# One split operation on 128 partitions with low halves carried by DMA, and a third staging tile for weight slices

## The chip, the cores and the metric

The kernel runs on one core of a Trainium2 chip. A core has TensorE (PE, matrix multiplication, with its weight loads shown as PEld), VectorE (DVE), ScalarE (ACT), GpSimd (POOL) and SyncE (SP), which here issues the DMA transfers, in the order in which they stand in its queue. Each engine works through its own instructions in order and waits for others through semaphores. On-chip data lies in a memory of 128 partitions; TensorE writes its sums to eight banks of a second memory. The metric is the device time of one execution, in microseconds (us).

## The reference

Attention with a causal mask and a bias that decays with a running sum, then two dense layers with different nonlinearities, in single precision:

```python
# 4 batches, 8 heads, 576 positions, 64 per head
scores = (1.0 / np.sqrt(D)) * np.matmul(q, k.transpose(0, 1, 3, 2))
cum = np.cumsum(np.maximum(s, 0.0), axis=-1)
bias = -(cum[:, :, :, None] - cum[:, :, None, :])
scores = np.where(causal, -1000000000.0, scores + np.minimum(bias, 0.0))
attn = softmax(scores); x = attn @ v          # 2304 tokens x 512
h = x @ w_in;  x = (h * np.cos(h)) @ w_out     # first expert layer, 512 -> 2048 -> 512
h = x @ w_in2; out = (np.maximum(h, 0) + np.log1p(np.exp(-np.abs(h)))) @ w_out2
```

The weights arrive in double precision.

## The kernel before

**Precision.** A product is made of three matmuls on operands that are split into a high half (a rounded copy) and a low half (the value less its high half): high x high, high x low, low x high. Splitting is the work of ScalarE (the copy) and VectorE (the subtraction).

**Attention** runs over 32 units (batch and head). Two neighbouring heads form a pair, which is loaded, split and kept together. `raw` (two buffers) takes the loaded keys on partitions 0 to 63 and queries on 64 to 127. `tbk` gets the keys' high halves on partitions 0 to 63 (L482) and low halves on 64 to 127 (L492), `tbq` the queries' low halves on 0 to 63 (L494) and high halves on 64 to 127 (L483), so one matmul over 128 partitions gives both mixed products. `tak` and `taq` get the high halves again, by DMA (L485, L486), with the running sums as further rows. These tiles lie in three slots inside the tile `wlate`, so the trace calls all of them `wlate`; the first pair is prepared apart. For each unit TensorE first makes scores once for their maxima (L510, VectorE takes masked maxima into `mx`; its other output `junk` is never read), then the scores again for the exponentials (L564), then the products with the values. L538 copies numerators and denominators out, a DMA writes them to `adram`; after every fourth unit the denominators are read back (`rd<-adram`), and VectorE takes their reciprocals (L591, L592), to be used when the expert layers' input is loaded (L620).

**Expert layers.** Tokens are taken in blocks of 512 (one of 256), hidden features in 16 chunks of 128. For a chunk TensorE makes the hidden values in one of four banks (operands `xh`, `xl`), ScalarE and VectorE apply the nonlinearity (L657 to L664 in the first layer, L669 to L676 in the second), the result is split into `ghi` (L298) and `glo` (L307), and TensorE adds the chunk's share of the output in the other four banks. L664 and L676 free a chunk's bank.

**Weights.** Each of the two layers has 32 half slices. A half slice (512 KB in double precision) is loaded into one of two tiles `stage`, and brought to single precision in one of two tiles `conv` by L422 (ScalarE) and L424, L426, L429 and L432 (VectorE); then L440 and L442 split it (shown as L298 and L307 or L308). L432 is the last to read the staging tile.

**What sets the order.** A planner written in Python (class `Planner`) gives each operation a due time `vt`, plays the program through with estimated durations, and so fixes the order on each engine; on the chip each engine keeps that order, whatever the real times are. A transfer's landing is reckoned as its issue, 640 ns, its bytes, and 770 ns more. Where TensorE would have nothing to do at the start, the planner puts warming matmuls on zeros (L376). Due times are in units of attention (`u + offset`, offsets in `TUNE`: split -0.462, maxima -0.4135, scores 1.63) or of chunks.

## Time and profile before

| | us |
|---|---|
| median of three runs | 1023.58 |
| lowest, highest | 1022.13, 1024.79 |
| the profiled execution | 1024.17 |
| its span in the trace | 1022.4 |
| TensorE busy in the span | 1006.6 (98%) |
| VectorE busy | 701.5 (69%) |
| ScalarE busy | 613.8 (60%) |
| GpSimd busy | 49.4 (5%) |
| all DMA | 95.31 MB in 45098 packets |

The span is the time from the first to the last instruction of the program; the execution took 1.8 us more than that. Busy shares of the whole span are means over very different stretches. TensorE's matmuls overlap, and their ends are modelled, so "busy" is not the same as working at its best; where an engine is late shows in the waits. A releaser of a wait is inferred from semaphores.

### The profile page before, as it was taken

What the parts mean: (1) busy time and instruction counts of PE and PEld (TensorE: products, weight loads), DVE (VectorE), ACT (ScalarE), POOL (GpSimd) and SP (SyncE); (2) the same over time, 40 slices, a digit from 0 to 9 for tenths busy, and PEclk for the clock granted to TensorE, in tenths of its full rate; (3) what the DMA queues carried; (4) which work ended last, traced back from release to release, by engine and by line L of the source; (5) the groups of instructions that cost most, each with busy time, mean ns of one, the idle gap of its engine ahead of it and who ended that gap; (6) DMA issues with size and microseconds to landing.
All of it is one profiled execution on the core that took longest, in us unless ns stands there. A gap on an engine that the chain in (4) does not pass through costs nothing.

```text
span 1022.4 us, 14520 instructions
## 1 busy us (share of the span) xinstructions
PE 1006.6 (98%) x5179; PEld 844.5 (83%) x5179; DVE 701.5 (69%) x1441; ACT 613.8 (60%) x1129; POOL 49.4 (5%) x67
## 2 busy tenths in 40 slices
PE   8999999999999999999999998999999999999998
PEld 7888788877888889988888886888888998888886
DVE  8799898969974545545458999975564756545553
ACT  4777777767765545555456668664455555554444
POOL 8112111100000000000000000000000000000000
PEclk9999999999999999999999999999999999999999
DMA  5766666773522222102014435310230200001001
GB/s 164 223 184 201 169 181 189 190 198 114 170 83 83 62 83 82 44 21 62 1 43 136 152 124 175 124 62 1 83 105 9 84 1 23 19 1 42 1 1 41
DMA packets 45098, 95.31 MB, mean 93 GB/s; under 512 B 7586, under 2 KB 14242, under 8 KB 45026
## 3 DMA queue, kind: packets, MB, share of 16 engines
q1 hardware_dynamic: 45026, 94.39, 30.4%
q8 instruction: 40, 0.66, 0.3%
q14 instruction: 32, 0.26, 0.1%
HBM read 66.87 MB, written 18.64 MB: 84 GB/s over the span
## 4 chain that ended last, share of the span: by engine, by line
PE 81%; DMA 8%; DVE 5%; ACT 3%; issue 2%; POOL 1%; SPq 0%; ACTq 0%; DVEq 0%; POOLq 0%
PE bank L321 80%; DMA stage<-w 5%; DMA adram<-num 2%; PE bank L376 1%; DMA rd<-adram 1%; DVE conv L429 1%; ACT conv L422 1%; DVE junk L510 1%; DMA raw<-adram 1%; DVE pf L664 0%; DVE conv L432 0%; DVE conv L426 0%; POOL wlate L329 0%; DVE glo L307 0%; ACT pf L564 0%
## 5 line engine op out<-in xcount | busy, mean ns | idle before, releaser
L321 PE MATMUL bank<-xh,wearly 128*128 128x512 f32 (+1 forms) x640 | 195.5, 371 | 3.8 <-DVE pf L664 3.8
L321 PE MATMUL bank<-ghi,wearly 128*128 128x512 f32 (+1 forms) x640 | 194.9, 370 | 1.3 <-ACT ghi L298 1.3
L321 PE MATMUL bank<-ghi,wlate 128*128 128x512 f32 (+1 forms) x640 | 193.4, 368 | 0.6 <-ACT ghi L298 0.6
L321 PE MATMUL bank<-xh,wlate 128*128 128x512 f32 (+1 forms) x640 | 193.6, 368 | 0.0
L298 ACT ACTIVATE ghi<-pf 128x512 fp32r<-128x512 f32 (+1 forms) x160 | 94.1, 588 | 145.8 <-DVE pf L676 97.5
L307 DVE TENSOR_TENSOR glo<-pf,ghi 128x512 fp32r<-128x512 f32 (+1 forms) x160 | 101.9, 637 | 78.2 <-ACT ghi L298 77.6
L321 PE MATMUL bank<-wlate 128*128 128x320 f32 (+9 forms) x576 | 149.4, 362 | 2.9 <-POOL xl L329 1.7
L321 PEld LDWEIGHTS bank<-xh,wearly 128*128 128x128 f32 x640 | 118.1, 190 | 24.9 <-DVE pf L664 4.5
L321 PEld LDWEIGHTS bank<-ghi,wearly 128*128 128x128 f32 x640 | 118.0, 190 | 21.8 <-ACT ghi L298 1.7
L321 PEld LDWEIGHTS bank<-ghi,wlate 128*128 128x128 f32 x640 | 117.2, 189 | 20.9 <-ACT ghi L298 1.0
L321 PEld LDWEIGHTS bank<-xh,wlate 128*128 128x128 f32 x640 | 117.2, 189 | 19.9
L321 PE MATMUL bank<-pf,vf 128*65 128x320 f32 (+4 forms) x448 | 126.4, 384 | 0.8 <-ACT pf L564 0.8
L321 PE MATMUL bank<-glo,wlate 128*128 128x512 f32 (+1 forms) x320 | 118.1, 369 | 1.2 <-DVE glo L307 1.2
L321 PE MATMUL bank<-glo,wearly 128*128 128x512 f32 (+1 forms) x320 | 118.5, 370 | 0.2 <-DVE glo L307 0.2
L321 PE MATMUL bank<-xl,wearly 128*128 128x512 f32 (+1 forms) x320 | 118.4, 370 | 0.0
L321 PE MATMUL bank<-xl,wlate 128*128 128x512 f32 (+1 forms) x320 | 117.7, 368 | 0.0
L672 DVE SCALAR_TENSOR_TENSOR bc<-pf 128x512 f32<-128x512 f32 (+1 forms) x80 | 51.0, 638 | 86.1 <-ACT pf L670 86.0
L321 PEld LDWEIGHTS bank<-wlate 128*128 128x128 f32 (+1 forms) x576 | 94.6, 192 | 17.9 <-DVE mx L510 2.8
L660 DVE SCALAR_TENSOR_TENSOR pf<-pf,pf 128x512 f32<-128x512 f32 (+1 forms) x80 | 50.8, 635 | 54.8 <-ACT pf L658 54.7
L510 DVE CUSTOM_DVE_ANT_0 junk<-bank,mask 128x384 bf16<-128x384 f32 (+3 forms) x192 | 81.8, 468 | 9.3 <-PE bank L321 7.8
L564 ACT ACTIVATE pf<-bank 128x256 f32<-128x256 f32 (+2 forms) x160 | 67.0, 431 | 33.1 <-PE bank L321 24.7
L669 ACT ACTIVATE pf<-bank 128x512 f32<-128x512 f32 (+1 forms) x80 | 44.3, 554 | 67.7 <-PE bank L321 65.1
(79 smaller groups left out, 1370.2 us busy)
## 6 DMA issues: line engine op xcount, KB each, us to landing
stage<-w SPq DMA_DIRECT2D x64, 512.0 KB
raw<-qk SPq DMA_DIRECT2D x15, 576.0 KB
wlate<-wlate SPq DMA_DIRECT2D x30, 288.0 KB
vf<-v SPq DMA_DIRECT2D x32, 160.0 KB
adram<-num SPq DMA_DIRECT2D x32, 146.2 KB
xdram<-num SPq DMA_DIRECT2D x18, 256.0 KB
out<-num SPq DMA_DIRECT2D x18, 256.0 KB
raw<-adram SPq DMA_DIRECT2D x32, 128.0 KB
```

The lines of the kernel that those rows point to most:

```text
L298: opts.append((ACT, act_t(n, psum), (lambda: A.activation(o, i, AF.Copy, scale=1.0 if scale is None else scale))))
L307: return [(DVE, dve_t(n), lambda: V.tensor_tensor(o, a, hi.bitcast(F32), op=ALU.subtract))]
L321: X.matmul(o, a, b, start=st, stop=sp, skip_group_check=skip)
L376: X.matmul(bank[7][:, 0:256], zero[:, 0:128], zero, start=True, stop=True)
L422: P.op(vs_ - 2, [(ACT, act_t(512), lambda cf=cf, pr=pr: A.activation(cf, pr[:, :, 1].bitcast(F32), AF.Abs))], r=[(("st", i), (tag, half))] ...
L429: P.op(vs_ + 1, [(DVE, dve_t(512), lambda cv=cv, pr=pr: V.scalar_tensor_tensor(cv, pr[:, :, 1], 0xC0000000, cv, op0=ALU.bitwise_and, op1=A ...
L510: P.op(tx + 1, [(DVE, dve_t(w, True) + DX, lambda bk=bk, off=off, w=w, mo=mo, col=col, pr=pr, jk=junk[i if x < 2 else x - 2]: V.tensor_ten ...
L564: P.op(tx + 3, [(ACT, act_t(wt, True) + AX, lambda pt=pt, bk=bk, wt=wt: A.activation(pt[:, :wt], bank[bk][:, :wt], AF.Exp))], r=[(("bank", ...
L660: P.op(te + 2, [(DVE, dve_t(n), lambda a0=a0, a1=a1: V.scalar_tensor_tensor(a1, a1, MAGIC, a0, op0=ALU.subtract, op1=ALU.subtract))], r=[( ...
L669: P.op(te, [(ACT, act_t(n, True), lambda a0=a0, hp=hp: A.activation(a0, hp, AF.Abs, scale=0.5))], r=hr, w=[(k0, (tg, "a"))])
L672: P.op(te + 2, [(DVE, dve_t(n), lambda a0=a0, a2=a2: V.scalar_tensor_tensor(a2, a0, 2.0, a0, op0=ALU.subtract, op1=ALU.mult, reverse0=True))],
```

## The change

There are five edits.

1. Queries now come on partitions 0 to 63 of `raw` and keys on 64 to 127 (the host swaps them). For all pairs but the first, one ScalarE copy over 128 partitions fills `tbk` (keys' high halves on 64 to 127; the queries' on 0 to 63 for the time being), a second fills `tbq` on 0 to 63. One VectorE subtraction over 128 partitions then replaces `raw` by its low halves, and two DMA transfers carry them to `tbk` (0 to 63) and `tbq` (64 to 127). The first pair keeps two subtractions.
2. The factor 1/8 moves from the queries' copies to the exponential; the running sums are multiplied by 8 to match.
3. There are three staging tiles in place of two, taken in turn; a load's due time is 1.2 half steps ahead in place of 0.7 (`STG`).
4. `junk` becomes a view of the tile `bc`, which is not in use in that phase.
5. The planner reckons a transfer's landing 1250 ns behind its bytes in place of 770.

```diff
+STG = 1.2
...
-                    o.end = dma_free + 770.0
+                    o.end = dma_free + 1250.0
...
-    stage = [T(f"stage{i}", [128, 1024], U32) for i in range(2)] if wide else []
+    stage = [T(f"stage{i}", [128, 1024], U32) for i in range(3)] if wide else []
...
-    junk = [T(f"junk{i}", [128, (384, 512)[i]], BF16) for i in range(2)]
+    junk = [bc[:, i, 0:256].bitcast(BF16) for i in range(2)]
...
-                sg = stage[i]
-                dma(at(f + half * 0.5 - 0.7), sg, wsrc.bitcast(U32), r=[("go", 0)], w=[(("st", i), (tag, half))])
+                j = (stage_n[0] - 1) % 3
+                sg = stage[j]
+                dma(at(f + half * 0.5 - STG), sg, wsrc.bitcast(U32), r=[("go", 0)], w=[(("st", j), (tag, half))])
...
-            P.op(t + (14 if u else 16), [(ACT, act_t(2 * S), lambda: A.activation(tbk[0:64, :, 0:S], raw[0:64], AF.Copy))], r=kr, w=[(ktbk, pt_)])
-            P.op(t + 15, [(ACT, act_t(2 * S), lambda: A.activation(tbq[64:128], raw[64:128], AF.Copy, scale=0.125))], r=kr, w=[(ktbq, pt_)])
...
+                P.op(t + 14, [(ACT, act_t(2 * S) + AX, lambda: A.activation(tbk[:, :, 0:S], raw, AF.Copy))], r=kr, w=[(ktbk, pt_), (ktbkl, (pt_, "h"))])
+                P.op(t + 15, [(ACT, act_t(2 * S) + AX, lambda: A.activation(tbq[0:64], raw[0:64], AF.Copy))], r=kr, w=[(ktbq, pt_)])
...
-            P.op(t + 18, [(DVE, dve_t(2 * S), lambda: V.tensor_tensor(tbk[64:128, :, 0:S], raw[0:64], hk, op=ALU.subtract))],
-                 r=kr + ([(ktbk, pt_)] if u else kk), w=[(ktbkl, pt_)])
-            P.op(t + 19, [(DVE, dve_t(2 * S), lambda: V.scalar_tensor_tensor(tbq[0:64], raw[64:128], 0.125, tbq[64:128].bitcast(F32), op0=ALU.mult, op1=ALU.subtract))],
-                 r=kr + [(ktbq, pt_)], w=[(ktbql, pt_)])
+                P.op(t + 18, [(DVE, dve_t(2 * S) + DX, lambda: V.tensor_tensor(raw.bitcast(F32R), raw, tbk[:, :, 0:S].bitcast(F32), op=ALU.subtract))],
+                     r=kr + [(ktbk, pt_), (ktbkl, (pt_, "h")), (ktbq, pt_)], w=[((kraw, x), (pt_, "l")) for x in range(2)])
+                lr = [((kraw, x), (pt_, "l")) for x in range(2)]
+                dma(t + 19, tbk.bitcast(F32)[0:64, :, 0:S], raw[64:128], r=lr, w=[(ktbkl, pt_)])
+                dma(t + 20, tbq.bitcast(F32)[64:128], raw[0:64], r=lr, w=[(ktbql, pt_)])
...
-            P.op(tx + 3, [(ACT, act_t(wt, True) + AX, lambda pt=pt, bk=bk, wt=wt: A.activation(pt[:, :wt], bank[bk][:, :wt], AF.Exp))],
+            P.op(tx + 3, [(ACT, act_t(wt, True) + AX, lambda pt=pt, bk=bk, wt=wt: A.activation(pt[:, :wt], bank[bk][:, :wt], AF.Exp, scale=0.125))],
```

The planner makes a new order out of this. Lines behind the first edit move down by one to seven: L422 becomes L424, L432 L434, L538 L545, L591 L598, L660 L667, L664 L671. The number behind a tile's name is its buffer; numbers move up by one from `stage` on where a tile was added.

SP's queue around the first read of the denominators, before:

```order
L283 DMA wlate<-wlate 64x2x576
L283 DMA vf_100<-v 128x320
L283 DMA wlate<-wlate 64x2x576
L283 DMA adram<-num_102 65x576
L283 DMA raw_85<-qk 128x1152
L283 DMA rd<-adram 128x1x18
L283 DMA vf_99<-v 128x320
```

The same place now:

```order
L284 DMA wlate<-wlate 64x2x576
L284 DMA adram<-num_103 65x576
L284 DMA wlate<-wlate 64x2x576
L284 DMA wlate<-raw_85 64x2x576
L284 DMA rd<-adram 128x1x18
L284 DMA wlate<-raw_85 64x1152
L284 DMA vf_100<-v 128x320
L284 DMA adram<-num_102 65x576
L284 DMA rdram<-rd 4x32x18
L284 DMA raw_85<-qk 128x1152
```

Between the write of the numerators and the read stood the load of a pair; now a high half and the first new low half stand there, and the load comes after.

ScalarE at the end of attention (`L538 num_102<-bank_70` is the copy of the last unit's last numerators, L657 the first chunk's first operation), before:

```order
L538 ACTIVATE num_102<-bank_72 65x256
L298 ACTIVATE xh_82<-raw_85 128x512
L564 ACTIVATE pf_98<-bank_69 128x256
L422 ACTIVATE conv_89<-stage_87 128x512
L298 ACTIVATE wearly<-conv_90 128x512
L538 ACTIVATE num_102<-bank_70 65x320
L657 ACTIVATE pf_95<-bank_65 128x512
```

The same place now:

```order
L545 ACTIVATE num_103<-bank_72 65x256
L299 ACTIVATE wearly<-conv_91 128x512
L571 ACTIVATE pf_99<-bank_69 128x256
L299 ACTIVATE xh_82<-raw_85 128x512
L424 ACTIVATE conv_90<-stage_88 128x512
L424 ACTIVATE conv_91<-stage_89 128x512
L545 ACTIVATE num_103<-bank_70 65x320
L664 ACTIVATE pf_96<-bank_65 128x512
```

Two reads of staging tiles stand ahead of the last numerators in place of one, and the split of a converted slice has moved ahead of the last exponential.

VectorE from the wait for the last denominators to the operation that frees the first chunk's bank, before:

```order
L591 TENSOR_SCALAR rd<-rd 128x18
L307 TENSOR_TENSOR xl_84<-raw_85,xh_82 128x512
L592 RECIPROCAL rd<-rd 128x18
L432 SCALAR_TENSOR_TENSOR conv_90<-stage_88,conv_90 128x512
L664 TENSOR_TENSOR pf_95<-bank_65,pf_97 128x512
```

The same place now:

```order
L598 TENSOR_SCALAR rd<-rd 128x18
L308 TENSOR_TENSOR wlate<-conv_91,wlate 128x512
L599 RECIPROCAL rd<-rd 128x18
L428 TENSOR_SCALAR conv_90<-conv_90 128x512
L667 SCALAR_TENSOR_TENSOR pf_99<-pf_99,pf_97 128x512
L671 TENSOR_TENSOR pf_96<-bank_65,pf_98 128x512
```

Four operations stand between the two where three stood.

## Rows read from the trace of the kernel before

**Rows 1.** Busy time by stretch (us: length, engines' busy time with instructions, clock, DMA).

```profile
0.00:26.00 26.00, 23.11 (x161) 18.57 (x162) 21.91 (x60) 12.12 (x15) 20.59 (x37) 0.93 0.57 166
26.00:212.00 186.00, 184.75 (x1155) 151.75 (x1153) 161.07 (x493) 138.00 (x302) 28.82 (x30) 1.00 0.69 190
212.00:240.00 28.00, 23.45 (x103) 18.70 (x102) 21.16 (x40) 18.53 (x35) 0.00 (x0) 0.94 0.58 165
240.00:528.00 288.00, 288.00 (x1453) 246.29 (x1452) 166.21 (x289) 161.33 (x292) 0.00 (x0) 1.00 0.21 68
528.00:640.00 112.00, 108.66 (x466) 88.10 (x465) 103.94 (x189) 80.79 (x141) 0.00 (x0) 0.98 0.44 145
```

Behind the stretch and its length come PE, PEld, DVE, ACT and POOL, then TensorE's granted clock, the DMA engines' share and GB/s.

**Rows 2.** Waits, 26 to 212 us (total us, times, longest us).

```profile
PEld bank L321 <- DVE mx L510: 2.8, 5, 0.9
PEld bank L321 <- DVE xl L516: 1.8, 5, 0.5
...
DVE rd L591 <- DMA rd<-adram: 4.3, 5, 1.2
```

**Rows 3.** VectorE's groups by shape, 26 to 212 us (busy us, mean ns | idle before).

```profile
L494 DVE SCALAR_TENSOR_TENSOR wlate<-raw,wlate 64x1152 fp32r<-64x1152 f32 x14 | 19.4, 1389 | 0.4
L492 DVE TENSOR_TENSOR wlate<-raw,wlate 64x1152 fp32r<-64x1152 f32 x13 | 17.9, 1375 | 0.4
...
L510 DVE CUSTOM_DVE_ANT_0 junk<-bank,mask 128x256 bf16<-128x256 f32 x29 | 12.3, 423 | 1.8 <-PE bank L321 1.0 <-ACT num L538 0.3 <-issue 0.2
...
L510 DVE CUSTOM_DVE_ANT_0 junk<-bank,mask 64x256 bf16<-64x256 f32 x29 | 11.9, 411 | 0.0
```

Each unit has one of the third and one of the fourth.

**Rows 4.** The chain of waits, 96 to 116 us (start, duration, what).

```profile
98.24 5.00 DMA adram<-num
...
103.30 2.54 DMA rd<-adram
...
110.78 1.36 DVE wlate L492
```

**Rows 5.** The chain of waits at the first handover, 212 to 234 us.

```profile
219.42 0.66 ACT conv L422
...
220.94 4.59 DMA adram<-num
...
225.59 4.41 DMA rd<-adram
...
230.03 0.18 DVE rd L591
...
231.51 0.61 DVE pf L664
```

**Rows 6.** Waits at the handovers: 212 to 240 us (two rows), 528 to 640 us (one).

```profile
ACT conv L422 <- DMA stage<-w: 9.1, 5, 2.5
...
PE bank L321 <- DVE pf L664: 3.8, 1, 3.8
...
ACT conv L422 <- DMA stage<-w: 12.2, 13, 1.9
```

**Rows 7.** TensorE in order of time, 600 to 645 us (idle before, releaser).

```profile
617.85 0.50 PE L321 MATMUL bank<-glo,wlate 128*128 128x512 f32 x1 [1.08 <-DVE glo L307]
...
630.08 0.51 PE L321 MATMUL bank<-ghi,wearly 128*128 128x512 f32 x1 [1.28 <-ACT ghi L298]
```

**Rows 8.** Busy time by stretch, 600 to 640 us, columns as in rows 1.

```profile
600.00:640.00 40.00, 36.83 (x152) 29.20 (x151) 38.20 (x70) 31.32 (x55) 0.00 (x0) 0.96 0.46 156
```

**Rows 9.** VectorE's groups by shape, 528 to 640 us.

```profile
L429 DVE SCALAR_TENSOR_TENSOR conv<-stage,conv 128x512 uint32<-128x512 uint32 x24 | 16.4, 685 | 0.2
```

**Rows 10.** What the DMA queues moved, 26 to 212 us.

```profile
DMA packets 17867, 35.42 MB, mean 190 GB/s; under 512 B 3921, under 2 KB 7633, under 8 KB 17847
```

**Rows 11.** TensorE in order of time, 0 to 30 us.

```profile
1.19 6.63 PE L376 MATMUL bank<-zero 128*128 128x256 bf16 x34 [1.19 <-DVE zero L334]
9.52 1.37 PE L321 MATMUL bank<-wlate 66*128 66x320 f32 x6 [1.69 <-POOL xl L329]
```

More of the change, by code (lines that the diff above doesn't have):

```diff
@@ L387, in build @@
     dma(vt, sraw, s, w=[(nk[0], "s")])
-    P.op(vt + 1, [(DVE, dve_t(S, fast=True), lambda: V.tensor_scalar_max(sraw, sraw, 0.0))], r=[(nk[0], "s")], w=[(nk[0], "spos")])
+    P.op(vt + 1, [(DVE, dve_t(S, fast=True), lambda: V.tensor_scalar(sraw, sraw, 0.0, 8.0, op0=ALU.max, op1=ALU.mult))], r=[(nk[0], "s")], w=[(nk[0], "spos")])
     P.op(vt + 2, [(DVE, dve_t(S), lambda: V.tensor_tensor_scan(cum, sraw, sraw, 0.0, op0=ALU.add, op1=ALU.bypass))],
@@ L422, in emit_weights @@
                     P.op(vs_ - 2, [(ACT, act_t(512), lambda cf=cf, pr=pr: A.activation(cf, pr[:, :, 1].bitcast(F32), AF.Abs))],
-                         r=[(("st", i), (tag, half))], w=[(("cv", i), (tag, half, -2))])
+                         r=[(("st", j), (tag, half))], w=[(("cv", i), (tag, half, -2))])
                     P.op(vs_ - 1, [(DVE, dve_t(512, fast=True), lambda cf=cf: V.tensor_scalar(cf, cf, HI_MIN, HI_MAX, op0=ALU.max, op1=ALU.min))],
@@ L427, in emit_weights @@
                     cv, hs, 3, 0x3FFFFFFF, op0=ALU.logical_shift_left, op1=ALU.bitwise_and))],
-                    r=[(("st", i), (tag, half))] + ([(("cv", i), (tag, half, -1))] if GUARD else []), w=[(("cv", i), (tag, half, 0))])
+                    r=[(("st", j), (tag, half))] + ([(("cv", i), (tag, half, -1))] if GUARD else []), w=[(("cv", i), (tag, half, 0))])
                 P.op(vs_ + 1, [(DVE, dve_t(512), lambda cv=cv, pr=pr: V.scalar_tensor_tensor(
                     cv, pr[:, :, 1], 0xC0000000, cv, op0=ALU.bitwise_and, op1=ALU.bitwise_or))],
-                    r=[(("st", i), (tag, half)), (("cv", i), (tag, half, 0))], w=[(("cv", i), (tag, half, 1))])
+                    r=[(("st", j), (tag, half)), (("cv", i), (tag, half, 0))], w=[(("cv", i), (tag, half, 1))])
                 P.op(vs_ + 2, [(DVE, dve_t(512), lambda cv=cv, pr=pr: V.scalar_tensor_tensor(
                     cv, pr[:, :, 0], 29, cv, op0=ALU.logical_shift_right, op1=ALU.bitwise_or))],
-                    r=[(("st", i), (tag, half)), (("cv", i), (tag, half, 1))], w=[(("cv", i), (tag, half))])
+                    r=[(("st", j), (tag, half)), (("cv", i), (tag, half, 1))], w=[(("cv", i), (tag, half))])
                 src = cv.bitcast(F32)
@@ L481, in emit_attention @@
                     t = at(-7.9)
-            P.op(t + (14 if u else 16), [(ACT, act_t(2 * S), lambda: A.activation(tbk[0:64, :, 0:S], raw[0:64], AF.Copy))], r=kr, w=[(ktbk, pt_)])
-            P.op(t + 15, [(ACT, act_t(2 * S), lambda: A.activation(tbq[64:128], raw[64:128], AF.Copy, scale=0.125))], r=kr, w=[(ktbq, pt_)])
-            if u:
-                dma(t + 16, tak.bitcast(F32)[0:64, :, 0:S], tbk.bitcast(F32)[0:64, :, 0:S], r=[(ktbk, pt_)], w=kk)
-                dma(t + 17, taq.bitcast(F32)[0:64, :, 0:S], tbq.bitcast(F32)[64:128], r=[(ktbq, pt_)], w=kq + ([("go", 0)] if u == 2 else []))
+                P.op(t + 14, [(ACT, act_t(2 * S) + AX, lambda: A.activation(tbk[:, :, 0:S], raw, AF.Copy))], r=kr, w=[(ktbk, pt_), (ktbkl, (pt_, "h"))])
@@ L487, in emit_attention @@
+                P.op(t + 15, [(ACT, act_t(2 * S) + AX, lambda: A.activation(tbq[0:64], raw[0:64], AF.Copy))], r=kr, w=[(ktbq, pt_)])
+                dma(t + 16, tak.bitcast(F32)[0:64, :, 0:S], tbk.bitcast(F32)[64:128, :, 0:S], r=[(ktbk, pt_)], w=kk)
+                dma(t + 17, taq.bitcast(F32)[0:64, :, 0:S], tbq.bitcast(F32)[0:64], r=[(ktbq, pt_)], w=kq + ([("go", 0)] if u == 2 else []))
                 dma(t + 16.5, tak.bitcast(F32)[64:66, :, 0:S], cdram[u:u + 2].rearrange("h t s -> t h s"),
@@ L488, in emit_attention @@
                     r=[(("cum", 0), 0), (("cum", 1), 0)], w=kg)
-            if u == 2:
-                t = at(st["sub1"])
-            hk = (tak[0:64, :, 0:S] if u == 0 else tbk[0:64, :, 0:S]).bitcast(F32)
-            P.op(t + 18, [(DVE, dve_t(2 * S), lambda: V.tensor_tensor(tbk[64:128, :, 0:S], raw[0:64], hk, op=ALU.subtract))],
-                 r=kr + ([(ktbk, pt_)] if u else kk), w=[(ktbkl, pt_)])
-            P.op(t + 19, [(DVE, dve_t(2 * S), lambda: V.scalar_tensor_tensor(tbq[0:64], raw[64:128], 0.125, tbq[64:128].bitcast(F32), op0=ALU.mult, op1=ALU.subtract))],
-                 r=kr + [(ktbq, pt_)], w=[(ktbql, pt_)])
+                if u == 2:
+                    t = at(st["sub1"])
@@ L772 @@
     kt = k.reshape(NB * NH, S, D).transpose(0, 2, 1)
-    qk = np.concatenate([kt, qt], axis=1).reshape(NB * NH // 2, 2, 2 * D, S).transpose(0, 2, 1, 3)
+    qk = np.concatenate([qt, kt], axis=1).reshape(NB * NH // 2, 2, 2 * D, S).transpose(0, 2, 1, 3)
     vp = np.zeros((NB * NH, 640, D), v.dtype)
```

10 lines of the change are left out of this document (8 added, 2 removed).

## Prediction

> **What bounds the kernel now.** I read the stretches of the span first, because a share of busy time over the whole run hides where time can be won. Rows 2 are the five that matter [rows 1]. From 240 to 528 us TensorE is busy 288.00 of 288.00 us at full granted clock: no edit on another engine can shorten that, and the long stretch behind 640 us is alike. The time that TensorE does not use lies elsewhere: 2.89 us idle in the first 26 us, 1.25 us in the attention phase (26 to 212), 4.55 us where attention hands over to the first expert layer (212 to 240, "first handover"), and 3.34 us where the second layer's weights are converted (528 to 640, "second handover"). At both handovers the mean granted clock is also below full, 0.94 and 0.98, that is, TensorE falls for a while from its level of 2.4 GHz towards 1.2 after it stood idle; that costs 28 x 0.06 = 1.7 us and 112 x 0.02 = 2.2 us. So the first handover loses 6.2 us, the second 5.5 us.
>
> Next come the waits, stretch by stretch. In attention TensorE's weight loads wait for VectorE's maxima, 2.8 + 1.8 = 4.6 us [rows 2], more than the idle time says, since a late load is partly hidden by the matmul before it. VectorE itself is busy 161.07 of 186 us. The chain of waits shows one such stall: a write of attention numerators to DRAM takes 5.00 us, the read of the denominators 2.54 us, VectorE stands at the line that wants them, and then has the two subtractions of the split (the first takes 1.36 us) in front of the maxima that TensorE wants [rows 4]. At the first handover the same two transfers end the chain, 4.59 and 4.41 us, VectorE waits at L591, and L664, which frees the bank, comes 1.48 us behind [rows 5]; TensorE stood 3.8 us for that [rows 6]. At both handovers ScalarE, which works in order, waits at L422 for a slice of weights: 9.1 us and 12.2 us [rows 6].
>
> **The change part by part.** *One subtraction for two.* Before, a pair of heads costs VectorE 1375 + 1389 ns on 64 partitions [rows 3]. The trace has no such operation on 128 partitions; the nearest rows are one masked maximum on 128 x 256 and on 64 x 256, 423 and 411 ns, so partitions do not set the time, and I take 1375 ns (at the worst 1375 x 423/411 = 1415). Fifteen pairs save 15 x 1389 ns = 20.8 us of VectorE; in the attention stretch its busy share goes from 0.87 to about 0.77. ScalarE keeps two copies per pair of the same length, and its cost does not move. On TensorE's path the ceiling is the 4.6 us of waits. A stall with a split in it goes, since 1.39 us is more than the longest single one, 0.9 us [rows 2]; a stall that comes from the denominators alone stays. The list of waits does not tell the two apart, so I take about half, 2.5 us, with bounds of 0 and 4.6.
>
> *The low halves by DMA.* Thirty transfers of 288 KB are added, and SP issues each of them behind the subtraction. They are wanted by the score matmuls, which stand 1.63 + 0.46 = 2.1 units behind the split in the planner's due times; a unit takes 186/29 = 6.4 us [rows 3], so 13 us. The longest transfer in my rows takes 5.0 us, which leaves some 8 us of cover: no cost. If that cover were gone, every pair would stall by the rest. Queued behind the new waits on SP are the next values, numerators, keys and queries; the first piece of the order shows the denominators' read between the two new transfers. The attention stretch moves 35.42 MB at a DMA share of 0.69 [rows 1, 10]; 26 more transfers are 7.7 MB, and at the same rate the share becomes 0.84. So the queue is fuller but not full, and I charge nothing, with the slower end below as a rival.
>
> The Trainium skill (SBUF — State Buffer, section "Door 1: The DMA port swizzle") says that a transfer on 64 partitions reaches only 8 of the 16 memory ports and so about half the rate, and that two such transfers do not add up to a whole one. No row here times one alone. With its asymptote of 218 GB/s, 7.7 MB would be an estimated 35 us of the stretch's 186, a share of 0.88 in place of 0.84: the sum stays, and only the rival's chance rises.
>
> *The planner's landing time.* It now reckons 480 ns more for each transfer. That costs nothing by itself; it puts the instructions that wait for a transfer later among their engine's others, so fewer of them block. VectorE's waits for denominators in attention, 4.3 us in five places [rows 2], should shrink; what of that reaches TensorE is in the 2.5 us.
>
> *The third staging tile.* In the second handover 24 half slices are converted in 112 us [rows 9], one in 4.7 us. With two tiles a load starts when the half two places back has been read; with three, one place earlier, so some 4.7 us sooner, more than the longest wait of 2.5 us [rows 6]. All 21 us of ScalarE's waits for slices should go. Next in line is VectorE: from 600 to 640 us it is busy 38.20 of 40 us [rows 8], and the conversion's work is unchanged, in nearly the same places among the chunks. TensorE's gaps there (1.08 us behind a low half, 1.28 us behind a high half [rows 7]) come from VectorE and ScalarE being late, and VectorE idled 8.06 us of the 112 before and among them [rows 1]. If half of that idle time is won as a lead, 4 us, it is more than the 3.34 us lost, and the clock stays up as well. Since VectorE stays near its limit I take 4.0 of 5.5 us, bounds 0 and 5.5.
>
> *The first handover.* The order of ScalarE shows two conversions now in front of the copy of the last numerators, where one stood; their slices were asked for earlier. The wait of 2.5 us in front of that copy goes, and one conversion, 0.66 us [rows 5], comes in. The 4.59 and 4.41 us of transfers stay, and VectorE has one operation more of the kind that takes 685 ns [rows 9] before it frees the bank. Net 2.5 - 0.66 - 0.69 = 1.2 us, bounds -1 (the transfers meet more traffic) and 2.5.
>
> *The start.* TensorE gets 127 warming matmuls for 123. Nine of the additions precede the first real matmul, where it waited 1.69 us for GpSimd [rows 11]; at 6.63/34 = 0.195 us each they take 1.76 us, so they are covered. Behind it there are five fewer, at most 5 x 0.195 = 1.0 us; I take half, 0.5 us, with bounds of -1.5 (the waits they covered show) and 2 (a subtraction less helps VectorE here too).
>
> Sum: 2.5 + 4.0 + 1.2 + 0.5 = 8.2 us. The profiled execution took 1024.17 us (span 1022.4), 0.59 us above the median of 1023.58. So 1024.17 - 8.2 = 1015.97, and against the median **1015.4 us**.
>
> **The rivals.** *VectorE still binds the second handover.* For it: 38.20 of 40 us, and the planner puts the conversions where they were. Against it: the idle time before. Then that term is 1.0 and the attention term 2.0: 1024.17 - 4.7 - 0.59 = 1018.9 us, and 1020.9 with no gain at the first handover and the start either (1024.17 - 2.7 - 0.59).
>
> *The DMA queue delays the denominators: slower.* The place is VectorE's wait at L591, once for every four heads, eight times in all. If both new transfers lie in front of both steps, each step is later by 0.59 MB at 35.42 MB / (186 us x 0.69) = 276 GB/s, 2.1 us, the two by 4.2 us. In attention VectorE waited 4.3 us there, and TensorE lost between 1.25 us (its idle time) and 4.6 us (the waits of its loads) [rows 1, 2], 0.3 to 1.1 of it; I count 0.5: 8 x 4.2 x 0.5 = 16.8 us. Less the 8.2 won, 8.6 us slower: 1032.2 us. It decides from 8.2/(8 x 0.5) = 2 us of added wait for each read. Against it: before, a load of 576 KB stood between the numerators and the denominators' read, and now two transfers of 288 KB do, the same bytes.
>
> *Everything at the handovers goes.* 4.6 + 5.5 + 6.2 + 0.5 = 16.8 us: 1006.8 us; it needs the 9.0 us of transfers in a row at the first handover to lie elsewhere, which the order speaks against.
>
> *Nothing reaches TensorE*, since another engine takes the place of each late one: about 1023 us.
>
> **How the numbers follow.** Forecast (a gain of 5 to 12 us) 0.56; VectorE binds 0.18; the queue delays 0.10; all goes 0.08; nothing reaches it 0.08. A measurement of this kernel tells about 0.3% from no change, 3.1 us; the bound is 1020.5 us. Faster: 0.56 + 0.08 + two thirds of 0.18 = 0.76. Same: the rest of 0.18, and most of 0.08: 0.13. Slower: 0.11. For the range I take the terms' better ends, without all of them at once (4.0 + 5.5 + 2.5 + 1.5 = 13.5 us, 1010.1 us), and on the other side the case of VectorE at 1020.9: from 1009.5 to 1021.5 us, which leaves out the queue's case, the two extremes and little else.
>
> **What the profile after would show.** Right: VectorE's busy time near 680 us; the attention stretch some 2 us shorter with a DMA share near 0.84; ScalarE's wait for slices near zero at both handovers; TensorE's gaps near 616 and 630 us gone, with the clock at full there; a gap of about 3 us still at the first handover, behind the denominators. Wrong: a longer wait for denominators in attention (the queue), a subtraction well above 1.4 us, score matmuls waiting for a transfer, or the gaps near 616 and 630 us unchanged while ScalarE no longer waits (VectorE binds).

## The result, and the profile after

The changed kernel takes **1037.65 us** (median of four runs, 1035.93 to 1038.52) against 1022.86 us for the kernel before beside it: a ratio of 1.0146, with a 95% interval of 1.0115 to 1.0178. It is slower by about 15 us where 8 us less were predicted. The profiled execution took 1038.1 us.

On its page, the first line and TensorE's:

```profile
span 1036.4 us, 14556 instructions
...
PE 1007.6 (97%) x5183; PEld 846.1 (82%) x5183; DVE 676.6 (65%) x1427; ACT 613.7 (59%) x1128; POOL 47.2 (5%) x67
```

TensorE's busy time has grown by 1.0 us only (1006.6 before); the span has grown by 14.0 us. So 13 us of the loss is time in which TensorE stands. The stretches, with the columns of [rows 1], say where:

```profile
0.00:26.00 26.00, 22.86 (x165) 18.60 (x166) 19.28 (x58) 12.55 (x17) 19.73 (x37) 0.93 0.68 195
26.00:212.00 186.00, 172.16 (x1063) 140.41 (x1061) 129.32 (x450) 125.12 (x277) 25.10 (x28) 0.98 0.85 219
212.00:240.00 28.00, 25.19 (x136) 20.23 (x135) 20.01 (x46) 17.62 (x42) 2.35 (x2) 0.88 0.68 187
240.00:528.00 288.00, 282.58 (x1419) 241.34 (x1418) 169.47 (x299) 163.21 (x293) 0.00 (x0) 0.99 0.24 77
528.00:640.00 112.00, 112.00 (x496) 92.75 (x495) 98.64 (x180) 81.53 (x139) 0.00 (x0) 1.00 0.38 124
```

From 26 to 212 us TensorE now stands for 13.84 us, where it stood for 1.25 [rows 1], and gets 1063 matmuls done for 1155. The DMA engines' share went from 0.69 to 0.85, just as the prediction said. The second handover (528 to 640 us) is full: its 3.34 us of idle time and the low clock are gone. Attention ends some 20 us later in the program than before, so the first handover has moved into the row that starts at 240 us; its 5.42 us of idle time is one gap.

What waits in attention, with the columns of [rows 2]:

```profile
DVE rd L598 <- DMA rd<-adram: 12.5, 6, 3.5
...
PEld bank L322 <- DVE xl L523: 7.8, 5, 2.7
...
PE bank L322 <- DVE xl L523: 5.4, 3, 2.2
...
PE bank L322 <- issue: 3.9, 2, 2.8
...
PEld bank L322 <- DMA wlate<-wlate: 3.0, 2, 2.5
PE bank L322 <- DMA wlate<-wlate: 2.9, 2, 2.3
```

VectorE's wait for denominators went from 4.3 to 12.5 us, and TensorE's largest gaps, 5.4 us, stand behind the maxima that VectorE takes after it (L523 gathers them). And something is new: TensorE itself waits for `wlate<-wlate`, the copies of *high* halves that were there before too and made nobody wait. The chain of waits shows both (start, duration, what; a transfer's duration runs from its issue to the release of what waited for it, and transfers that nothing waited for are not in a chain):

```profile
80.36 6.55 DMA adram<-num
...
86.98 2.10 DMA rd<-adram
...
89.09 0.18 DVE rd L598
...
94.39 8.00 DMA wlate<-wlate
...
102.43 5.47 PE bank L322 x24
...
120.51 8.57 DMA wlate<-wlate
```

Write and read of the denominators' way take 8.65 us here, where [rows 4] had 7.54. (Over the whole stretch such a pair of transfers stands in the chain six times, with 7.0 to 9.3 us, 8.3 in the mean; in the chain of before three times, with 6.2 to 7.5, 6.7 in the mean.) A copy of high halves takes 8.0 to 8.6 us; in the chain of before none stands. The maxima stand behind them; TensorE's own row, and SyncE's queue at the second copy:

```profile
102.43 0.47 PE L322 MATMUL bank<-wlate 66*128 66x320 f32 x2 [2.30 <-DMA wlate<-wlate]
```

```profile
120.51 1.36 SPq L284 DMA_DIRECT2D wlate<-wlate  x2
121.97 1.05 SPq L284 DMA_DIRECT2D adram<-num  x1
123.10 2.42 SPq L284 DMA_DIRECT2D wlate<-raw  x2
...
127.90 0.33 SPq L284 DMA_DIRECT2D adram<-num  x1
133.36 0.34 SPq L284 DMA_DIRECT2D raw<-qk  x1
```

The `wlate<-raw` are the new transfers. SyncE then stands from 128.2 to 133.4 us before the next load into the same buffer of `raw`: that load may not start until the low halves have been read out of it. From 26 to 212 us SyncE waits 13 times for these transfers. In the kernel before it stood for the second subtraction instead (L494), 17.6 us in 9 places.

```profile
SPq L284 <- DMA wlate<-raw: 31.5, 13, 5.4
```

Whatever comes behind in SyncE's queue stands with it. But the chain from 26 to 212 us goes through none of these waits, and no wait of TensorE is put down to `wlate<-raw` (3.9 us of its waits have no releaser named). What is plainly late are the other transfers, after their issue.

At the first handover the chain has other transfers than in [rows 5], and the gap is longer than the 3.8 us of [rows 6]:

```profile
231.38 5.99 DMA stage<-w
...
238.53 5.77 DMA raw<-adram
...
248.11 2.96 DMA raw<-adram
...
252.07 0.61 DVE pf L671
```

```profile
252.72 0.80 PE L322 MATMUL bank<-xh,wearly 128*128 128x512 f32 x1 [5.42 <-DVE pf L671]
```

### The profile page after: what moved, and what is told of

Its sections match the earlier page's. It is cut to its first block, busy times and chain, and to the rows that moved or that the text cites. A ratio compares the mean times of both kernels' runs of the same rounds, so it can differ in the third digit from the quotient of the medians.

```text
span 1036.4 us, 14556 instructions
## 1 busy us (share of the span) xinstructions
PE 1007.6 (97%) x5183; PEld 846.1 (82%) x5183; DVE 676.6 (65%) x1427; ACT 613.7 (59%) x1128; POOL 47.2 (5%) x67
## 4 chain that ended last, share of the span: by engine, by line
PE 87%; DMA 9%; ACT 1%; issue 1%; DVE 1%; POOL 1%; SPq 0%; DVEq 0%; ACTq 0%; POOLq 0%
PE bank L322 86%; DMA adram<-num 3%; DMA rd<-adram 2%; DMA wlate<-wlate 2%; PE bank L377 1%; DMA raw<-adram 1%; DMA raw<-rdram 1%; DMA stage<-w 1%; ACT pf L571 0%; POOL wlate L330 0%; SPq L284 0%; DMA vf<-v 0%; ACT wlate L491 0%; DVE raw L627 0%; DVE rd L598 0%
## 5 line engine op out<-in xcount | busy, mean ns | idle before, releaser
L322 PE MATMUL bank<-pf,vf 128*65 128x320 f32 (+4 forms) x448 | 129.9, 391 | 0.0
L322 PEld LDWEIGHTS bank<-wlate 128*128 128x128 f32 (+1 forms) x576 | 97.2, 197 | 27.5 <-issue 7.6
L517 DVE CUSTOM_DVE_ANT_0 bc<-bank,mask 128x256 bf16<-128x256 f32 (+4 forms) x192 | 82.0, 470 | 28.0 <-PE bank L322 18.7
L667 DVE SCALAR_TENSOR_TENSOR pf<-pf,pf 128x512 f32<-128x512 f32 (+1 forms) x80 | 50.8, 635 | 57.2 <-ACT pf L665 57.2
```

The costliest lines, as they stand in the source:

```text
L322: X.matmul(o, a, b, start=st, stop=sp, skip_group_check=skip)
L517: P.op(tx + 1, [(DVE, dve_t(w, True) + DX, lambda bk=bk, off=off, w=w, mo=mo, col=col, pr=pr, jk=junk[i if x < 2 else x - 2]: V.tensor_ten ...
L667: P.op(te + 2, [(DVE, dve_t(n), lambda a0=a0, a1=a1: V.scalar_tensor_tensor(a1, a1, MAGIC, a0, op0=ALU.subtract, op1=ALU.subtract))], r=[( ...
```

## The experiments

**The theory** after this reading (A): the 30 added transfers fill the queue, and what is late is everything else that goes through it. **The rivals**: the planner's new order is at fault (B); SyncE, which works in order, stands for the subtraction ahead of each new transfer (C); the third tile loads weights earlier, into the busy time (D). Runs were measured in groups, each with the kernel before beside them, which took 1021.3 to 1023.0 us; ratios are against it in the same group, with 95% intervals in brackets, and differences are taken between ratios.

**1. The bytes taken out, the order kept.** From the fourth pair on, each transfer of low halves carries 4 partitions of 64; the copy of the high halves writes only its own 64 partitions, and the planner still reckons the full bytes.

```diff
-                dma(t + 19, tbk...[0:64, :, 0:S], raw[64:128], r=lr, w=[(ktbkl, pt_)])
-                dma(t + 20, tbq...[64:128], raw[0:64], r=lr, w=[(ktbql, pt_)])
+                lp = 64 if pt_ < 3 else 4     # planned as if 64
+                dma(t + 19, tbk...[0:lp, :, 0:S], raw[64:64 + lp], r=lr, w=[(ktbkl, pt_)])
+                dma(t + 20, tbq...[64:64 + lp], raw[0:lp], r=lr, w=[(ktbql, pt_)])
```

> The changed kernel with every instruction in its place on every engine; only the two transfers that carry the low halves are cut from 64 partitions to 4 from the fourth pair of heads on (36 KB in place of 576 KB for each of 13 pairs), so that the low halves of most rows are stale and the scores are not the reference's. The copy of the high halves then writes 64 partitions in place of 128, at the same length per partition. Theory A (the bytes: the added transfers keep the queue at 0.85 of its time and make the copies of high halves and the denominators' reads late): the attention stretch comes back, 1038 less the 16 to 21 us that it lost there: 1016 to 1022 us, DMA share in 26 to 212 us back near 0.70, VectorE's waits for denominators back near 4 us, no wait of TensorE for a transfer of high halves above 1 us. Theory B (the planner's new order, by the landing time and the third tile): the order is the same, so 1035 to 1040 us. Theory C (SyncE works in order, and stands for the subtraction in front of each of the two transfers, whatever they carry): also 1033 to 1040 us, with the share at 0.70.

Measured: 1017.55 us, ratio 0.9956 (0.9938 to 0.9973): 1.9% or 19 us below the changed kernel. The attention stretch is back:

```profile
26.00:212.00 186.00, 183.34 (x1161) 152.06 (x1160) 143.73 (x484) 140.79 (x307) 27.58 (x30) 1.00 0.73 199
```

The one copy of high halves that stands in its chain takes 6.3 us:

```profile
85.91 6.32 DMA wlate<-wlate
```

So the loss goes with the bytes. B falls, since the order is the same on every engine. C falls for these 19 us: SyncE still waits for every subtraction here. One thing this run does not separate: bytes can cost by making the other transfers slower (A), or by holding SyncE before the next load into `raw`, and that stand shrinks with the bytes too, from 31.5 us:

```profile
SPq L284 <- DMA wlate<-raw: 10.4, 5, 3.5
```

For A speaks the chain of the changed kernel, which has slow transfers in it and no such stand.

**2. The split without tile and landing time.** The diff is that of the change without `STG`, the third tile, `junk` and the 1250.

> The split by one operation with the low halves by DMA alone: two staging tiles, the slice asked for 0.7 of a half ahead and a landing time of 770 ns, as before. Theory A: the loss in attention is all there and the gain at the second handover is not: 1038 + 5.5 to 6.7 = 1043 to 1045 us, high-half copies of 8 us, waits at the second handover as before. Theory B (the planner's order): near the kernel before or a little faster, 1018 to 1025 us. Theory C: like A, 1043 to 1045 us.

Measured: 1049.54 us, ratio 1.0258 (1.0233 to 1.0283). So the split alone costs 26 us on the kernel before. That is some 5 us more than expected; a landing time of 770 ns that is worse for it than 1250 would fit (run 11 goes on from there), but this run does not show it apart from the third tile. The DMA share in attention is 0.78 here, lower than the changed kernel's 0.85, at a larger loss.

**3. The third tile alone**, with the load's due time of 1.2 half steps (`STG`).

```diff
-    stage = [T(f"stage{i}", [128, 1024], U32) for i in range(2)] if wide else []
+    stage = [T(f"stage{i}", [128, 1024], U32) for i in range(3)] if wide else []
-    junk = [T(f"junk{i}", [128, (384, 512)[i]], BF16) for i in range(2)]
+    junk = [bc[:, i, 0:256].bitcast(BF16) for i in range(2)]
...
```

> The third staging tile alone (three tiles, the slice asked for 1.2 ahead, the maxima's scratch in bc), with the two subtractions, 64-partition layout and the landing time of 770 ns of before. Theory A and C: 1023 less the second handover's 5.5 to 6.7 us = 1016 to 1018 us, attention as before (1.3 us idle from 26 to 212 us), ScalarE's wait for slices at the second handover under 1 us. Rival D (the third tile's earlier loads are what fills the queue in attention): 1025 to 1032 us with attention 5 to 10 us worse and the DMA share there above 0.75.

Measured: 1016.35 us, ratio 0.9942 (0.9923 to 0.996). TensorE is busy 112.00 of 112 us in the second handover and stands 2.24 us in attention; D falls.

```profile
528.00:640.00 112.00, 112.00 (x495) 92.74 (x495) 110.58 (x206) 86.32 (x149) 0.00 (x0) 1.00 0.49 158
```

**4. The landing time alone.**

```diff
-                    o.end = dma_free + 770.0
+                    o.end = dma_free + 1250.0
```

> The kernel before with the planner's landing time of 1250 ns in place of 770 and nothing else: only the order moves. Theory A and C: 1020 to 1025 us, within 0.3% of before. Theory B (the landing time gives a worse order): 1030 to 1040 us, with VectorE or TensorE waiting behind moved work in attention.

Measured: **1010.26 us**, ratio 0.9879 (0.986 to 0.9898). No theory expected that: 12 us won by one number in the planner. In attention TensorE stands 0.15 us, and at the second handover, with two tiles, ScalarE waits 2.2 us for slices where [rows 6] had 12.2:

```profile
26.00:212.00 186.00, 185.85 (x1170) 154.73 (x1170) 162.86 (x499) 140.92 (x311) 28.86 (x30) 1.00 0.70 192
```

```profile
ACT conv L422 <- DMA stage<-w: 2.2, 4, 0.8
```

VectorE's wait for denominators in attention falls from 4.3 to 0.7 us:

```profile
DVE rd L591 <- DMA rd<-adram: 0.7, 1, 0.7
```

The transfers carry the same bytes; what needs one stands later in its engine's order, behind work that can go on. The first place where VectorE's two orders differ is such a one: a conversion of weights has moved ahead of L591.

**5. Third tile and landing time together, without the split.** This is what the split must be charged against.

> The changed kernel without the split: three staging tiles, the slice asked for 1.2 ahead, landing time 1250 ns, and the two subtractions on 64 partitions of before. It is what the split is to be charged against. The landing time alone gave 1010.3 us and the third tile alone 1016.4, and both emptied the second handover (its 6.7 us), so the two gains overlap there: theory A (the split is the whole loss): 1006 to 1011 us. Rival (the third tile and the landing time get in each other's way, with slices loaded earlier in attention): 1015 to 1025 us.

Measured: 1012.83 us, ratio 0.9915 (0.9896 to 0.9934). That is above the 1006 to 1011 us expected. The two gains overlap, as both empty the second handover: run 4 has TensorE busy 112.00 of 112 us there with two tiles. More than that, with 1250 ns the third tile does not pay: this run is 0.36%, 3.7 us (1 to 6), slower than run 4. The changed kernel is 1.0146 - 0.9915 = 2.3%, or 24 us, above it: that is the price of the split in this order.

**6 and 7. Does it matter who waits for them, and their shape?** From the fourth pair on the new transfers go to scratch columns of `xh`, 256 KB each: once from 64 partitions, once from 128. The low halves used are stale, and the planner reckons the transfers as before.

```diff
+                    if pt_ >= 3:                      # run 6: 64 partitions of 4 KB
+                        dst = xh[1].bitcast(F32)[64 * y:64 * y + 64, 1:3].rearrange("p a c -> p (a c)")
+                        src = src.rearrange("p h s -> p (h s)")[:, 0:1024]
...
+                        dst, src = xh[1].bitcast(F32)[:, 1 + y], raw[:, y, 0:512]   # run 7: 128 of 2 KB
```

> The changed kernel in its order, where from the fourth pair on the two transfers of low halves (64 partitions, 288 KB each) go to scratch columns of xh, 64 partitions and 256 KB each, so nothing waits for their landing and the low halves used are stale. If the score matmuls' wait for the low halves' landing is what costs: near the thin transfers' 1017.6 us (1016 to 1021). If the bytes cost by delaying the other transfers: 1033 to 1038 us, as the changed kernel, less a little for 11% fewer bytes.

> As the run before, with the same 256 KB in each scratch transfer but spread over 128 partitions of 2 KB in place of 64 of 4 KB. If it is the 64-partition shape that makes the transfers slow (the Trainium skill, SBUF — State Buffer, section Door 1: The DMA port swizzle, has such a transfer reach half of the ports): about halfway or nearer to the thin transfers, 1018 to 1027 us, with a DMA share in 26 to 212 us of 0.78 to 0.80. If only the number of bytes counts: the same time as the 64-partition run within 2 us, and the same share, 0.83 to 0.85.

Measured: 1036.18 us, ratio 1.0136 (1.0106 to 1.0165), and 1030.41 us, 1.0082 (1.0063 to 1.0102). The attention rows, of 64 and then of 128 partitions:

```profile
26.00:212.00 186.00, 173.04 (x1042) 141.20 (x1040) 127.15 (x440) 126.90 (x272) 23.94 (x27) 0.95 0.82 213
```

```profile
26.00:212.00 186.00, 173.69 (x1072) 142.01 (x1071) 131.17 (x455) 130.14 (x281) 24.53 (x28) 0.98 0.82 220
```

In run 6 nothing waits for the landing of these transfers, except the next load into `raw` and the next transfer to the scratch (SyncE stands 20.4 us for them from 26 to 212 us), and the loss is there as before. So the wait of the score matmuls, the only one for which the prediction had looked for cover, is not what costs. Of the 18 us between run 6 and the thin transfers (1.0136 - 0.9956), 5.5 us go with the shape (1.0136 - 1.0082, an interval of 2 to 9 us) and 13 us with the bytes; neither of the two expectations for run 7 was met. The shape's part has the sign that the Trainium skill (SBUF — State Buffer, section "Door 1: The DMA port swizzle") gives it, but not the size that a halved rate would suggest: the DMA share is 0.82 in both, at 213 and 220 GB/s.

**8. The denominators put later.** Their read and the two operations on them are due one unit later, for all but the last four heads.

```diff
-        tn = at(st["norm"])
+        tn = at(st["norm"] + (1.0 if u < 28 else 0.0))
```

> The changed kernel with the denominators' read, addition and reciprocal put one unit (one head) later in the planner's due times for all but the last four heads; every transfer is as it was. In the changed kernel VectorE waits 12.5 us for these reads from 26 to 212 us, and TensorE has gaps of 2.2, 1.5, 2.2 and 1.0 us behind them, 6.9 us. If those waits carry the loss: 1029 to 1033 us, with VectorE's wait for denominators under 4 us. If the queue is simply short of time (share 0.85) or the high halves' copies carry it: the gaps come back behind other transfers, 1035 to 1040 us.

Measured: 1029.28 us, ratio 1.0085 (1.0053 to 1.0116): 6 us less than the changed kernel (2 to 11 us). VectorE still waits 7.6 us for the denominators, where under 4 were expected, and TensorE now 3.2 us at a time for a copy of high halves. So the denominators carry a part of the loss, and the rest comes back behind the next late transfer.

**9. The converse: the bytes added to the kernel without the split.** Two scratch transfers of 256 KB in each pair from the fourth on, in the kernel of run 5.

```diff
+                        for y in range(2):
+                            nc.sync.dma_start(xh[1]...[64 * y:64 * y + 64, 1:3]..., raw[64 - 64 * y:128 - 64 * y]...[:, 0:1024])
```

> The converse: the kernel with third tile, landing time of 1250 ns and the two subtractions (1012.8 us), every instruction in its place, and from the fourth pair on two more transfers of 256 KB from raw to scratch columns of xh, 64 partitions each, right behind the copy of the queries' high halves. Nothing waits for their landing and SyncE does not wait for a subtraction in front of them. If the bytes alone carry the loss: 1028 to 1034 us (1012.8 plus the 18.6 us between the scratch and the thin transfers), share in 26 to 212 us from 0.70 to about 0.82, longer waits of VectorE for denominators. If it takes SyncE's wait for the subtraction or the order of the split: 1013 to 1019 us.

Measured: 1041.13 us, ratio 1.0187 (1.0145 to 1.0229): 28 us above run 5, more than expected, with VectorE's wait for the denominators at

```profile
DVE rd L603 <- DMA rd<-adram: 20.5, 6, 6.5
```

Neither the subtraction nor the order of the split is needed for the loss, then: the added transfers are enough. But the run is not as clean as was expected. Something does wait for them, SyncE, before its next load into `raw` or transfer to the scratch:

```profile
SPq L284 <- DMA xh<-raw: 50.4, 13, 6.3
```

And here such a stand is in the chain, with the denominators' read issued right behind it:

```profile
108.99 5.96 DMA xh<-raw
...
115.08 0.33 SPq L284
...
115.51 3.51 DMA rd<-adram
```

Nor does the planner know of these transfers. The share in attention is 0.77, not the 0.82 expected:

```profile
26.00:212.00 186.00, 171.08 (x1028) 139.04 (x1027) 143.92 (x450) 124.43 (x270) 27.15 (x28) 0.96 0.77 203
```

So added transfers cost in two ways, by slower transfers beside them and by holding SyncE until their source is free; what each is worth was not measured apart.

**10. Another issuing engine.**

```diff
-            nc.sync.dma_start(o, i)
+            q.dma_start(o, i)          # nc.scalar for the two low halves
```

> The changed kernel with the two transfers of low halves issued by ScalarE in place of SyncE, at the same places of the program, with the same bytes. If SyncE's standing for the subtraction, or the order in SyncE's one queue, makes the others late: 1022 to 1031 us, with shorter denominators' reads and copies of high halves. If the DMA engines' time itself is short: 1033 to 1040 us; and slower than 1040 us if ScalarE, which works in order, now stands for the subtraction.

Measured: 1046.37 us, ratio 1.0223 (1.0199 to 1.0247): slower still, and past the 1040 us of the third expectation. VectorE's wait for denominators is 15.2 us and TensorE's longest for high halves 5.1 us, so a queue of its own does not take the new transfers out of the others' way. This agrees with the Trainium skill (DMA: Bandwidth & Descriptors, section "Issuing engines are not separate DMA queues"), by which all issuers share the same 16 engines. Whether ScalarE also stood for the subtraction was not separated, and SyncE still stands 29.7 us for the low halves to leave `raw`. The run gives one more number, since the low halves have a queue of their own (q10), beside all other transfers from 26 to 212 us (q1):

```profile
q1 hardware_dynamic: 15019, 30.72, 61.1%
q10 hardware_dynamic: 2924, 7.69, 17.6%
```

7.69 MB in 0.176 x 186 us of the 16 engines is 235 GB/s, against 30.72 / (0.611 x 186 us) = 270 GB/s for all others, the 64-partition copies of high halves among them: 13% less.

**11. The changed kernel with a later planned landing.** 2500 ns in place of 1250.

> The changed kernel with the planner's landing time at 2500 ns in place of 1250, so that what waits for a transfer stands later among its engine's instructions; the transfers are the same. If the loss is latency that another order can cover: 1018 to 1030 us, with waits of VectorE for denominators and of TensorE for high halves mostly gone, at the same share near 0.85. If the queue is short of time whatever the order: 1034 to 1040 us.

Measured: 1018.95 us, ratio 0.9968 (0.9947 to 0.9988): 18 us won back, with every byte still there and a *higher* share:

```profile
26.00:212.00 186.00, 175.91 (x1098) 144.71 (x1096) 135.72 (x468) 129.45 (x288) 23.46 (x28) 0.99 0.89 230
```

```profile
DVE rd L598 <- DMA rd<-adram: 7.7, 4, 3.6
PE bank L322 <- DMA wlate<-wlate: 6.7, 3, 3.7
```

```profile
90.09 6.95 DMA wlate<-wlate
...
102.86 9.94 DMA wlate<-wlate
```

The transfers are no faster (7 to 10 us for a copy of high halves). SyncE stands 33.4 us for the low halves, no less than before. What changed is how much of all that the order covers.

**12. The kernel before with 2000 ns.**

> The kernel before with a landing time of 2000 ns. At 770 it takes 1023 us and at 1250 it took 1010.3 us, with the waits of VectorE for denominators in attention down from 4.3 to 0.7 us. If the gain comes from waits that the order covers, most is had at 1250 already: 1007 to 1013 us. If 1250 was a lucky order and no trend: anywhere from 1010 to 1023 us.

Measured: **1007.31 us**, ratio 0.9845 (0.9825 to 0.9865), the lowest of all that ran, with the two subtractions and the two staging tiles of before. The chain of waits from 26 to 212 us, by line, is TensorE and next to nothing else:

```profile
by line: PE bank L321 98.4%; DMA stage<-w 2.6%; ACT pf L564 0.2%; SPq L283 0.1%; issue 0.1%; ACTq L564 0.0%
```

**13 and 14. What the split is worth where the order allows for the landing.** At 2500 ns: third tile with the two subtractions, and the changed kernel with thin transfers.

> Third staging tile, the two subtractions of before, landing time 2500 ns: the counterpart without the split of the changed kernel at 2500 ns (1018.95 us). At 2000 ns and two tiles the kernel takes 1007.3 us. If the split costs even where the order covers the landing: 1005 to 1009 us, so that the split is charged 10 to 14 us in place of 24.8. If 2500 ns is past the best: 1012 to 1020 us.

> The changed kernel with the low halves' transfers cut to 4 of 64 partitions from the fourth pair on, landing time 2500 ns: one subtraction for two, with nearly no bytes for it. Against the two subtractions at the same landing time it prices the relief of VectorE by itself, which the prediction put at 2.5 us (0 to 4.6). If that relief is worth what the prediction said: 2 to 3 us faster than the run before. If it is worth nothing, since the order already covers VectorE's late work: within 2 us of it, or slower by the steps that the split puts in a row (copy, subtraction, transfer).

Measured: 1011.05 us, ratio 0.9895 (0.9876 to 0.9915), and 1009.96 us, 0.9889 (0.9869 to 0.9909). At this landing time the whole split costs 0.9968 - 0.9895 = 0.7%, 7.5 us, in place of 24. With its bytes gone it is 0.6 us better than two subtractions, with an uncertainty of about 3 us: no gain can be told, though the 2.5 us of the prediction is not excluded. At 1250 ns the same pair (runs 1 and 5) stands at 0.9956 to 0.9915, 4 us *against* one subtraction.

**15 and 16. Where the trend ends.** The changed kernel at 4000 ns, the kernel before at 3000.

> The changed kernel with the landing time at 4000 ns. At 1250 it takes 1037.7 and at 2500 it took 1019.0 us, with 10.3 us of TensorE's gaps left in attention, most behind copies of high halves. If an order can hide the rest too: 1008 to 1014 us. If the queue (share 0.89 at 2500 ns) is now the bound of the stretch: 1015 to 1021 us, no shorter than 2500 ns gave.

> The kernel before with a landing time of 3000 ns. 770, 1250 and 2000 ns gave 1023, 1010.3 and 1007.3 us. If the waits that an order can cover are used up at 2000 ns (one wait of 0.5 us for denominators is left in attention): 1005 to 1010 us. If a later place costs the engines that come behind: 1010 to 1016 us.

Measured: 1019.56 us, ratio 0.9974 (0.9961 to 0.9987), and 1008.73 us, 0.9873 (0.9855 to 0.9891). Neither is better than at 2000 or 2500 ns, and they are 1.0%, 10 us, apart; some 2 of these go with the third tile (run 13 beside run 16), which only the changed kernel has. So with the split no landing time that was tried reached the two subtractions. At 4000 ns attention itself has less left to win, with 3.78 us of idle time where run 11 had 10.09, at the same share of 0.89. Part of the rest lies at the first handover, as the rows from 212 to 240 us show, first with the split (run 15), then without (run 13):

```profile
212.00:240.00 28.00, 23.96 (x102) 18.54 (x100) 22.99 (x44) 18.52 (x35) 0.00 (x0) 0.88 0.73 204
```

```profile
212.00:240.00 28.00, 27.36 (x126) 22.27 (x125) 25.95 (x51) 22.41 (x39) 0.00 (x0) 1.00 0.65 197
```

## Why the prediction was wrong

**Low halves by DMA, charged at nothing: the step that failed.** The added bytes cost 19 us (run 1), the split as a whole 24 (run 5). The share was forecast right, 0.84 against 0.85 measured. The mistake was in what was made of it. "The queue is fuller but not full" asks whether the bytes fit; what mattered is how long the transfers beside them then take from issue to landing. In the chains copies of high halves took 8.0 to 8.6 us (6.3 in run 1), the denominators' two transfers 8.3 us for 6.7, and each has readers of its own. The prediction also had no term for SyncE, which waits 31.5 us for the low halves' transfers (run 1: 10.4); what of that reaches TensorE stays open, as the chain of the changed kernel shows none of it and that of run 9 does. The cover was worked out for one reader, the score matmuls, 8 us of it, and run 6 shows that even with that reader gone the loss stays. The 8 us of cover itself also came from a transfer of 5.0 us timed in the emptier queue, a write of half the bytes (146 KB).

**The rival of the slow queue** had the sign, the place and nearly the size: 1032.2 us, with a chance of 0.10. Its waits for denominators did grow, from 4.3 to 12.5 us in attention, but the two transfers came 1.6 us later and not 4.2, less than the 2 us from which it was to decide; they were only one of the carriers (run 8: 6 us), and the copies of high halves, which the rival did not name, another. The argument against it, "the same bytes" between numerators and read, looked at one place of SyncE's order, while the bytes were added all over the stretch. In the rival beside it, VectorE at the second handover, a sum is wrong: with 1.0 and 2.0 us won the second time is 1024.17 - 3.0 - 0.59 = 1020.6, not 1020.9 us; the measured time lies far outside the range with either.

**The landing time, "costs nothing by itself".** True as to cost, wrong as to size: alone it is worth 12 us (run 4), the largest gain in the change. The prediction saw the mechanism (fewer instructions block) and put it into the attention term's 2.5 us. Its reading had the numbers: a chain with transfers of 4 to 5 us [rows 4, 5] beside a planner that reckoned 0.77 us past the bytes. In the profile of run 4 TensorE's idle time is 6.0 us less (1.1 in attention, 1.9 at the first handover, 3.3 at the second, and the start lost 0.3), and its busy time 7.2 us less for the same work (999.4 for 1006.6). Part of the latter is the granted clock, 1.00 where it was 0.93 at the start and 0.98 at the second handover; the rest would be delay inside busy rows: the weight loads' waits for VectorE in attention, 4.6 us before, are 1.0 us now. The prediction took half of those 4.6 us, gave it to the subtraction, and priced the other terms one by one, without a term for what the new order does in all stretches at once.

**Attention, 2.5 us from one subtraction for two.** The operation came out as taken (1354 ns on 128 partitions against 1375 predicted), and VectorE's busy time too (676.6 us against "near 680"). But runs 13 and 14 leave no gain that can be told, and run 4 emptied the same waits with both subtractions in place: VectorE's work was not what held TensorE, its waits in order were.

**The second handover, 4.0 us of 5.5.** Right in mechanism for the third tile alone, and a little small: it gives 0.58%, 5.9 us in all (run 3), the clock there is 1.00, and TensorE does not stand though VectorE is busy 110.58 of 112 us. The rival that VectorE binds fell. In the change as a whole the term is not the tile's: the landing time alone fills that stretch, and the tile on top of it costs 3.7 us (run 5).

**The first handover, a gain of 1.2 us: wrong sign.** TensorE's gap went from 3.8 to 5.42 us. The case of the lower bound, transfers that meet more traffic, came, with loads of 5.8 to 6.0 us in the chain, and went past its -1 us.

**The start, 0.5 us.** Nothing in these runs times it apart; TensorE's idle time to 26 us is 3.14 us against 2.89, within the bound.

Put together: all but the split gives 0.85%, 8.7 us (run 5). That this is near the 8.2 of the sum is luck: 2.5 of these were for the split, the tile's 4.0 fall to the landing time, and the landing time had no term. The charge of nothing, in truth 24 us, turned the sign.

## What to carry to other kernels

The DMA share of a stretch was no measure of slack here: the three slowest runs (2, 9 and 10) have 0.77 to 0.79 from 26 to 212 us, where they also get fewer matmuls done, and run 11, with 18 us less than the changed kernel, has 0.89. Before adding transfers, ask for each of the *other* transfers in the queue who waits for it and with how much cover, and what the issuing engine must hold back until the new ones are done. Work moved from VectorE, which had idle time, to the shared queue was paid here by those behind that queue. Where a schedule is fixed in advance, compare the landing times that it assumes with those in the chain of waits first: here that one number was worth more than the split and the third tile, and it took away what the tile gains.

## What the runs showed that had not been expected

- How long one and the same transfer takes from issue to landing is no constant: a copy of 288 KB in the chains of attention took 6.3 us in run 1 (share 0.73), 8.0 to 8.6 in the changed kernel (0.85), 7.0 to 9.9 in run 11 (0.89). These are copies that something waited for; a rule by the share is not shown, as a copy took 8.0 us in run 10 too (0.79).
- The bytes that were moved set the larger part of the cost, the 64-partition shape about a third (runs 6 and 7), and a 64-partition copy ran at 235 GB/s of the engines' time beside 270 for the rest (run 10).
- The gaps are not all of the cost: with the waits came a mean granted clock of 0.98 from 26 to 212 us (0.94 in run 2), 0.88 from 212 to 240 us and 0.99 from 240 to 528 us, where the kernel before had 1.00, 0.94 and 1.00. TensorE's busy time for the same instructions is 1007.6 us, and 1001.2 in run 1.
